# First batch of a cosformer attention and routed FFN kernel: the order of loading, scaling and summing is rearranged

## The chip, the cores and the metric

The kernel runs on one core of a Trainium2 chip. The metric is the device time of one execution in microseconds (us). Four runs of the kernel before took 980.68, 981.9, 982.14 and 980.2 us, a median of 981.29. One execution was recorded by the hardware profiler.

## The reference

A linear attention is followed by a soft mixture of eight experts. N = 8 x 576 = 4608 tokens of width 512 come out of the attention, and all experts work on all tokens, weighted by a matrix P that is balanced in eight steps.

```python
batch, n_heads, seq, head_dim = (8, 8, 576, 64)
theta = np.pi / 2.0 * pos / S
def phi(x, c, s):
    r = np.maximum(x, 0.0)
    return np.concatenate([r * c, r * s], axis=-1)
q_p = phi(q, cos_w, sin_w); k_p = phi(k, cos_w, sin_w)
kv = np.einsum('bhsf,bhsd->bhfd', k_p, v)
z = np.sum(k_p, axis=2)
num = np.einsum('bhsf,bhfd->bhsd', q_p, kv)
den = np.einsum('bhsf,bhf->bhs', q_p, z)[..., None] + 1e-06
x = (num / den)            # as (4608, 512)
P = np.exp(x @ w_gate)     # then 8 times: rows and columns normalized
for e in range(8):
    h = np.maximum(x @ w1[e], 0.0)
    out += P[:, e:e + 1] * (h @ w2[e])
```

## The kernel before

The chip's engines each run a stream of instructions in order: TensorE (PE), VectorE (DVE), ScalarE (ACT), GpSimd (POOL, here mostly the queue from which loads are issued) and SyncE (SP, here the queue of transposes and stores). The helpers te, ve and se record every operation in the order in which the source has it, so that the source order is the engines' order; that is why nearly all instructions of the profile carry line 109, and are told apart by the tiles that they write and read.

One core holds all of the attention's output as xT (512 columns on 4 x 128 partitions, by tokens). The attention runs batch by batch. Two heads form a pair hk (0 to 3), and a batch has two halves of two pairs each, one load for each of q, k and v and half, issued by `load` (L198). While batch b is attended to, expert 0's FFN works on tokens of the batches before: `ffn1` (L142, x by w1, relu into hT) and `ffn2` (L155). The list `todo`, filled at L651 to L728, hangs attention steps of later batches behind the FFN's slots. After the eighth batch come the other seven experts, from about 180 us to the end, in a form of Strassen's products; the change does not touch them.

Batch 0 has nothing to run beside, and its steps stand written out at L593 to L649. The names that matter:

- `load` order at L217 to L243: q0, then an iota (gidx, the positions) and a mask (ident, the identity), then q1, k0, k1, v0, v1, two quarters of w1, the two loads of batch 1's k, the other quarters, batch 1's q and v, and w2 in quarters. From the tenth load on, each waits for the one eight places ahead.
- `keep_busy(n)` (L245) gives TensorE matmuls whose result nobody reads, in all n x 128 columns wide. Before the first real work stand 74 of 128 columns.
- `cs` are the cosine and sine tables, made by ScalarE (L272); `cs_half` (L274 to L280) is a copy of the cosines of each half of the partitions, wanted by `key_sums`.
- `prep_q` (L346) multiplies a pair's q by cs on VectorE into q_p (a product of 128 x 1152; three buffers). `turn` (L389) transposes a third of that on TensorE into a bank of small_ps, of which there are four in rotation, and a relu takes it out into q_pT, on ScalarE for batch 0, alternately on ScalarE and VectorE for batch 1.
- `prep_k` (L339) is the relu of a pair's k in place, on VectorE for batch 0 and on either for batch 1; `prep_kp` (L375) its product with cs into k_p.
- `key_sums` (L412): z of a half's heads by 36 narrow matmuls straight from k; `key_sums_made` (L427) brings it into zsel on VectorE.
- `denominators` (L496): q_pT by zsel into one bank (three matmuls for each head), and with the last head the reciprocal `den`, its parts hi and hl, all on VectorE.
- `sums_begun` and `sums_made` (L446, L468): kv of a half by 36 matmuls into two banks, copied to kv_sb by ScalarE.
- `attend` (L531): for one pair, three matmuls spread hl over the partitions into two banks (rb_ps), ScalarE copies them to rb, four matmuls make the numerators into two more banks (num_ps), and VectorE multiplies both into xT.
- L623 to L647: four banks first_ps (two of h_ps, two of y_ps) collect the FFN's first four output tiles over kt = 0 to 3, each kt as soon as the pair hk = kt has been attended to, and then ScalarE takes the relus. `ffn1` of tile 4 and 5 uses the two banks of h_ps next.
- Between the attends stand the relus and products of batch 1's keys (L642 to L647), and behind them batch 1's q (L648).

The softmax here doesn't subtract the row's maximum and nothing guards it: scores larger than these inputs give would overflow.

## Time and profile before

| What | us |
|---|---|
| median of four runs | 981.29 |
| the profiled execution | 980.68 |
| its span, first to last instruction | 979.0 |

The stages of the profiled execution, with the busy time of each engine in them; a matmul's recorded length includes its way through the array, so that a busy PE is not a PE at its peak:

| us from the start | PE | DVE | ACT | POOL | GB/s |
|---|---|---|---|---|---|
| 0 to 8 | 6.86 | 4.12 | 4.12 | 6.79 | 94 |
| 8 to 16 | 7.99 | 5.94 | 4.81 | 4.59 | 191 |
| 16 to 24 | 7.75 | 6.43 | 4.83 | 4.07 | 203 |
| 24 to 34 | 8.24 | 7.47 | 8.62 | 4.52 | 206 |
| 34 to 44 | 10.00 | 7.35 | 5.58 | 0.00 | 184 |
| 44 to 80 | 34.79 | 27.62 | 23.62 | 8.57 | 161 |
| 80 to 180 | 100.00 | 66.62 | 60.02 | 14.50 | 128 |

The granted TensorE clock is 1.00 in each of them. Batch 0's own steps and batch 1's preparation fill the first 34 us. The loads of the start land one after another: q0 4.6 us after its issue at 1.31, q1 5.2 after 2.62, k0 7.3 after 3.39, k1 some 8 after 4.10. In these first microseconds PE is occupied by the 74 matmuls of 128 columns (1.14 to 7.94).

### The profile page before, as it was taken

To read this page: it belongs to the slowest core of one execution; us is meant where nothing else is said; L and a number is where in the kernel's file an instruction comes from. 1 tells how busy PE (TensorE), PEld (TensorE's weight loads), DVE (VectorE), ACT (ScalarE), POOL (GpSimd) and SP (SyncE) were. 2 spreads that over 40 slices of the span, in tenths; PEclk is the share of its full clock that TensorE was granted. 3 is DMA by queue.
4 is the path that set the end of the run, shared out by engine and by line. 5 is a ranking of instruction groups with operands and counts; after the bars stand their busy time and mean duration, and the time that the engine had idled before them with its cause. 6 is when DMAs were issued, how large, how long until landed. Compare 5 with 4: busy or idle time off the path is not lost.

```text
span 979.0 us, 20237 instructions
## 1 busy us (share of the span) xinstructions
PE 964.9 (99%) x7855; PEld 674.7 (69%) x7855; DVE 807.2 (82%) x1833; ACT 564.9 (58%) x1262; POOL 60.7 (6%) x82
## 2 busy tenths in 40 slices
PE   9999999999999999999999999999999999999997
PEld 6544454457777777777777777777777777777775
DVE  6767774888988888988888888988888888988887
ACT  5766665467776555555555555555555555555551
POOL 6231110010000000000000000000000000000001
PEclk9999999999999999999999999999999999999999
DMA  9999885330103401223103401223103401104435
GB/s 164 184 154 174 155 136 105 74 68 25 50 25 70 91 25 28 64 56 68 44 25 75 85 25 34 62 55 69 41 25 76 84 25 35 40 26 120 127 88 128
DMA packets 80336, 73.54 MB, mean 75 GB/s; under 512 B 33264, under 2 KB 72176, under 8 KB 80240
## 3 DMA queue, kind: packets, MB, share of 16 engines
q0 software_dynamic: 27232, 30.94, 20.3%
q1 hardware_dynamic: 52768, 41.06, 17.1%
q8 instruction: 61, 1.00, 0.4%
q14 instruction: 35, 0.29, 0.1%
q10 hardware_dynamic: 240, 0.26, 0.1%
HBM read 83.12 MB, written 12.98 MB: 98 GB/s over the span
## 4 chain that ended last, share of the span: by engine, by line
PE 88%; DMA 4%; DVE 3%; issue 2%; ACT 1%; POOL 1%; POOLq 0%; ACTq 0%; SPq 0%
PE rows_ps L109 33%; PE h_ps L109 26%; PE p_ps L109 11%; PE copied_ps L109 11%; PE y_ps L109 4%; PE small_ps L109 3%; DMA k_ld<-in_k_dram 1%; DMA w2e<-in_moe_w_dram 1%; DMA w1e<-in_moe_w_dram 1%; DMA acc_hi<-q_p 1%; DVE P_tok L109 1%; DVE colp L109 0%; POOL q_ld L202 0%; DVE rs L109 0%; DVE acc_hi L926 0%
## 5 line engine op out<-in xcount | busy, mean ns | idle before, releaser
L926 DVE SCALAR_TENSOR_TENSOR acc_lo<-rows_ps,P_tok,acc_lo 128x512 f32<-128x512 f32 (+1 forms) x322 | 203.5, 641 | 74.9 <-PE rows_ps L109 74.8
L109 PEld LDWEIGHTS <-H 128*128 128x128 f16 x2080 | 203.1, 98 | 82.5 <-issue 1.2
L862 ACT CAST u<-h_ps 128x384 f16<-128x384 f32 x288 | 137.8, 478 | 131.2 <-PE h_ps L109 131.2
L109 PEld LDWEIGHTS <-w1e 128*128 128x128 f16 x1632 | 157.3, 98 | 67.5 <-issue 5.9
L856 DVE CUSTOM_DVE_ANT_0 H<-p_ps,u 128x384 f16<-128x384 f32 x329 | 181.3, 551 | 6.4 <-PE p_ps L109 6.4
L109 PEld LDWEIGHTS <-hs 128*128 128x128 f16 x1500 | 146.6, 98 | 56.2
L109 PE MATMUL h_ps<-S,w1e 128*128 128x384 f16 x672 | 164.1, 326 | 0.7 <-ACT u L109 0.6
L109 PE MATMUL p_ps<-xT,T 128*128 128x384 f16 x672 | 164.1, 326 | 0.1
L109 PE MATMUL rows_ps<-V,H 128*128 128x256 f16 x1000 | 150.0, 273 | 0.7 <-DVE acc_hi L926 0.7
L109 PE MATMUL rows_ps<-w2e,hs 128*128 128x256 f16 x1000 | 150.0, 273 | 0.0
L109 PE MATMUL h_ps<-xT,w1e 128*128 128x384 f16 (+1 forms) x616 | 149.4, 350 | 0.3 <-DVE xT L109 0.2
L894 ACT ACTIVATE H<-h_ps 128x384 f16<-128x384 f32 x144 | 70.7, 491 | 95.0 <-PE h_ps L109 95.0
L109 PEld LDWEIGHTS <-T 128*128 128x128 f16 x1008 | 98.4, 98 | 29.9 <-issue 3.3
L109 PE MATMUL rows_ps<-w2e,H 128*128 128x256 f16 (+1 forms) x568 | 92.3, 285 | 0.0
L875 ACT COPY copied_ps<-h_ps 128x384 f32<-128x384 f32 x144 | 67.5, 468 | 35.2 <-PE h_ps L109 35.2
L885 ACT ACTIVATE H<-copied_ps 128x384 f16<-128x384 f32 x144 | 70.9, 492 | 20.3 <-PE copied_ps L109 20.3
L109 PE MATMUL h_ps<-S,T 128*128 128x384 f16 x336 | 81.8, 325 | 0.3 <-ACT copied_ps L109 0.3
L109 PE MATMUL copied_ps<-xT,w1e 128*128 128x384 f16 x336 | 82.1, 326 | 0.0
L109 PE MATMUL copied_ps<-w2e,H 128*128 128x256 f16 x504 | 75.5, 272 | 0.0
L109 PE MATMUL rows_ps<-V,hs 128*128 128x256 f16 x500 | 74.9, 272 | 0.0
L926 DVE SCALAR_TENSOR_TENSOR acc_lo<-copied_ps,P_tok,acc_lo 128x256 f32<-128x256 f32 x126 | 60.2, 478 | 0.4
L926 DVE SCALAR_TENSOR_TENSOR acc_hi<-rows_ps,P_tok,acc_hi 128x512 f32<-128x512 f32 (+1 forms) x56 | 41.3, 738 | 20.5 <-PE rows_ps L109 19.7
(145 smaller groups left out, 950.2 us busy)
## 6 DMA issues: line engine op xcount, KB each, us to landing
S<-x_saved SPq DMA_DIRECT2D x108, 192.0 KB, 2.4
out_dram<-acc_lo SPq DMA_DIRECT2D x62, 128.0 KB, 2.4
w1e<-in_moe_w_dram POOLq DMA_DIRECT2D x7, 1024.0 KB, 8.9
w2e<-in_moe_w_dram POOLq DMA_DIRECT2D x7, 1024.0 KB, 10.0
q_ld<-in_q_dram POOLq DMA_DIRECT2D x16, 288.0 KB, 6.4
k_ld<-in_k_dram POOLq DMA_DIRECT2D x16, 288.0 KB, 8.1
v_ld<-in_v_dram POOLq DMA_DIRECT2D x16, 288.0 KB, 9.4
x_saved<-S SPq DMA_DIRECT2D x18, 192.0 KB, 1.9
```

Of the source, the lines that this page charges most:

```text
L109: i = getattr(self.engine, name)(*args, **kwargs)
L856: latest = ve._custom_dve(TENSOR_ADD_SAT, out=out, in0=ps[:, 0:TU], in1=t[:], s0=FP32_MAX, s1=0.0)
L862: se.copy(out=t[:], in_=ps[:, 0:TU])
L875: se.copy(out=Y[:, 0:TU], in_=X[:, 0:TU])
L885: se.activation(out=h11, in_=Y[:, 0:TU], func=AF.Relu)
L894: se.activation(out=h12, in_=X[:, 0:TU], func=AF.Relu)
L926: ve.scalar_tensor_tensor(out=a, in0=rows, scalar=P_tok[:, g, self.e : self.e + 1], in1=a, op0=ALU.mult, op1=ALU.add,)
```

## The change

It rearranges batch 0 in these places:

1. POOL issues q0, q1, the iota, k0, the mask, k1, then as before.
2. `cs_half` is filled by a function `halve`, called behind the second q product instead of at once. Five small constants and the memsets of v_augs are made earlier.
3. All four q products stand ahead of the first relu of k (before, the fourth stood behind two relus).
4. Behind the turns come: the first key product, the first zsel, the two other key relus, the second key product, the first denominators, the second key sums, two wide fillers, the second zsel and denominators with the reciprocal, kv of half 0, five wide fillers, and only then the last two key products.
5. `attend` is split into `spread_out` and `numerators`. Pair 0 is attended to, two fillers follow, pair 1's spread, then kv of half 1, which goes into the two banks of h_ps instead of small_ps, two more fillers, and pair 1's numerators.
6. The four tiles of first_ps are worked on, and their relus taken, in the order 2, 3, 0, 1.
7. Batch 1's key relus on ScalarE (pairs 0 and 1) stand behind pair 3's copies, and all of batch 1's other key preparation behind the last attend.

The numbers of matmuls, relus and products stay the same but for the fillers (31 x 128 columns behind the turns before, 44 x 128 after).

```diff
         load(0, 0, "q")
+        load(0, 1, "q")
         gidx = cs_pool.tile([P, C], FP32, name="gidx")
...
+        load(0, 0, "k")
         ones_sq = cs_pool.tile([P, P], F16, name="ones_sq")
...
-        load(0, 1, "q")
-        for name in "kv":
-            load(0, 0, name)
-            load(0, 1, name)
+        load(0, 1, "k")
+        for half in range(2):
+            load(0, half, "v")
...
-        def sums_begun(b, half):
+        def sums_begun(b, half, banks=(ps_s, "small_ps")):
...
-            kv_ps = [ps_s.tile([P, 512], FP32, name="small_ps") for hh in range(2)]
+            kv_ps = [banks[0].tile([P, 512], FP32, name=banks[1]) for hh in range(2)]
...
         for hk in range(HK):
+            prep_q(0, hk)
+            if hk == 1:
+                halve()
             if hk == 3:
                 prep_k(0, 0)
                 prep_k(0, 1)
                 z_ps = key_sums(0)
-                prep_q(0, hk)
-                key_sums_made(0, z_ps)
-            else:
-                prep_q(0, hk)
             for i in range(3):
                 turn(0, hk, i, True)
                 keep_busy(3)
         prep_kp(0, 0)
+        key_sums_made(0, z_ps)
+        for hk in (2, 3):
+            prep_k(0, hk)
         prep_kp(0, 1)
         denominators(0, range(0, 4))
+        z_ps = key_sums(1)
         keep_busy(8)
+        key_sums_made(1, z_ps)
+        denominators(0, range(4, 8))
+        sums_made(0, 0, sums_begun(0, 0))
+        keep_busy(20)
         for hk in (2, 3):
-            prep_k(0, hk)
-        z_ps = key_sums(1)
-        prep_kp(0, 2)
-        key_sums_made(1, z_ps)
-        prep_kp(0, 3)
-        keep_busy(5)
-        denominators(0, range(4, 8))
-        for half in range(2):
-            sums_made(0, half, sums_begun(0, half))
-            keep_busy((0, 18)[half])
+            prep_kp(0, hk)
+        spread_out(0, 0)
+        numerators(0, 0)
+        keep_busy(8)
+        spread_out(0, 1)
+        sums_made(0, 1, sums_begun(0, 1, (ps_h[0], "h_ps")))
+        keep_busy(8)
...
         for hk in range(HK):
-            attend(0, hk)
+            if hk > 1:
+                spread_out(0, hk)
+            if hk:
+                numerators(0, hk)
+            if hk == 3:
+                prep_k(1, 0)
+                prep_k(1, 1)
             for kt in ((), (0,), (1,), (2, 3))[hk]:
-                for ft, h_ps in enumerate(first_ps):
+                for ft, h_ps in ((2, first_ps[2]), (3, first_ps[3]), (0, first_ps[0]), (1, first_ps[1])):
...
-            for i in ((), (0,), (1, 2), ())[hk]:
-                prep_k(1, i, i < 2)
-            for i in ((), (0,), (1,), (2, 3))[hk]:
-                if i == 3:
-                    prep_k(1, i, False)
-                prep_kp(1, i)
+        for hk in range(HK):
+            if hk >= 2:
+                prep_k(1, hk, False)
+            prep_kp(1, hk)
         for hk in range(3):
             prep_q(1, hk)
```

## The prediction

> **What bounds the kernel now.** I read the page first, then the stages, then each engine's timeline from 10 to 34 us, then who waits for whom after 34 us. The page says that over the whole span TensorE is the limit:

> ```profile
> PE 964.9 (99%) x7855; PEld 674.7 (69%) x7855; DVE 807.2 (82%) x1833; ACT 564.9 (58%) x1262; POOL 60.7 (6%) x82
> ```

> That average hides the start. The change touches only batch 0 and the preparation of batch 1, all before 34 us, and there the limit passes from engine to engine. VectorE (start, length, instruction, repeats, idle time before and its cause):

> ```profile
> 10.71 0.53 DVE L109 TENSOR_SCALAR k_ld<-k_ld 128x576 f16<-128x576 f16 x2 [1.78 <-DMA k_ld<-in_k_dram]
> 11.15 0.75 DVE L109 TENSOR_TENSOR q_p<-q_ld,acc_hi 128x1152 f16<-128x1152 f16 x1
> ...
> 15.82 1.35 DVE L109 RECIPROCAL den<-y_ps 96x192 f32<-96x192 f32 x1
> ...
> 17.50 0.41 DVE L109 SCALAR_TENSOR_TENSOR hl<-hi,lo,den 96x192 f16<-96x192 f16 x1
> 18.86 0.82 DVE L109 TENSOR_TENSOR xT<-small_ps,rb 128x384 f16<-128x384 f32 x2 [0.94 <-ACT rb L109]
> ...
> 24.96 0.30 DVE L109 TENSOR_SCALAR k_ld<-k_ld 128x576 f16<-128x576 f16 x1
> 25.29 0.76 DVE L109 TENSOR_TENSOR k_p<-k_ld,acc_hi 128x1152 f16<-128x1152 f16 x1
> 25.96 2.09 DVE L109 TENSOR_TENSOR q_p<-q_ld,acc_hi 128x1152 f16<-128x1152 f16 x3
> 27.97 0.55 DVE L109 TENSOR_SCALAR q_pT<-small_ps 128x384 f16<-128x384 f32 x1
> 28.44 0.75 DVE L109 TENSOR_TENSOR q_p<-q_ld,acc_hi 128x1152 f16<-128x1152 f16 x1
> 29.11 0.56 DVE L109 TENSOR_SCALAR q_pT<-small_ps 128x384 f16<-128x384 f32 x1
> ```

> The reader is to see prices here (a product of 1152 takes 0.75 us, but three take 2.09, so they start 0.67 apart; a relu with its product takes 0.33 more), and that VectorE goes without idle time from the first batch-1 products to the eviction at 29.11. TensorE and ScalarE in the same stretch:

> ```profile
> 17.97 0.42 PE L109 MATMUL small_ps<-hl,acc_hi 96*128 96x192 f16 x3
> ...
> 19.47 0.57 PE L109 MATMUL small_ps<-q_pT,kv_sb 128*64 128x384 f16 x4
> ...
> 24.42 0.59 PE L109 MATMUL h_ps<-xT,w1e 128*128 128x512 f16 x2 [0.24 <-DVE xT L109]
> 25.48 1.89 PE L109 MATMUL h_ps<-xT,w1e 128*128 128x512 f16 x8
> 27.21 0.67 PE L109 MATMUL small_ps<-ident,q_p 128*128 128x128 f16 x9
> ```

> ```profile
> 24.84 1.08 ACT L109 ACTIVATE hT<-h_ps 128x512 f16<-128x512 f32 x2 [1.34 <-PE h_ps L109]
> ...
> 26.76 1.24 ACT L109 ACTIVATE hT<-h_ps 128x512 f16<-128x512 f32 x2
> ...
> 32.54 0.73 ACT L109 COPY acc_lo<-v_ld 128x576 f16<-128x576 f16 x1
> ```

> From 24.84 to 33.27 us ScalarE has no idle row over 0.02 us: whatever delays the first relu of hT, or makes a hole behind it, delays the copy at 32.54, the key sums of batch 1 that wait for it, and all that follows.

> **The change part by part.** Loads: on POOL's queue q1 is issued ahead of the iota and k0 ahead of the mask. Each issue is some 0.72 us, so the iota and with it the cosine tables come 0.72 us later (3.67 instead of 2.95, done by 5.0), and q0 lands only at 5.9 (issue 1.31 plus 4.6 to landing): hidden, cost 0; without that cover it would be 0.72. VectorE begins q_p near 5.9 instead of 6.83, as it no longer waits for the table to fill cs_half. But TensorE's 74 warm-up matmuls and the three epsilon products end at 8.33, and the turns start there before and after: gain 0. No DMA of SP's moves.

> q ahead of k: the fourth q_p runs near 9.4 instead of 11.15, and the first key product takes its place. TensorE's row is unchanged to 13.16, because k0 lands at 10.68 and the key sums stand between the turns. What is gained is 0.67 us of VectorE. The next two key relus then run at 12.4 instead of 13.72, and the second key sums follow the first denominators at 13.60 without a wait, where they began at 14.14. Second denominators, reciprocal and hl come 0.5 us earlier: reciprocal 15.3, hl done 17.4, spread at 17.45 instead of 17.97. **So far -0.5.** Five fillers of 0.22 stand under the reciprocal, free while it lasts.

> The two key products now follow hl: 17.35 to 18.7 (0.67 + 0.75). The first xT multiplication, ready at 18.35, waits for them: 18.7 instead of 18.86. TensorE meanwhile: spread 0.35, numerators 0.37, two fillers 0.43, spread 0.34, half of 72 key-value products (1.15 us from 15.71 to 16.86) 0.58, two fillers 0.43, which is 2.50. Second numerators at 17.45 + 2.50 = 19.95 instead of 19.47: **the head start is gone and +0.45 stands.** The numerators take 0.37 instead of 0.50 (their bank is free by then), so the first h matmuls run at 20.3 for 19.97. Two rounds of 1.585 follow, unchanged. The last xT pair no longer stands behind a key product: 0.51 us after its rb copy (as 18.35 to 18.86) instead of 0.76, so it ends at 24.46 and kt = 3 starts at 24.5 for 24.42: **+0.1.** ScalarE's two key relus, moved here, take 23.7 to 25.0 and meet the first hT relu at 24.92.

> Now two things come late. First, ffn1(4) takes the buffer of first_ps[0], whose relu is now third of four: relus start 0.48 apart and last 0.60, so it is free 1.57 us after the first at 24.95, at 26.5 instead of 25.43. ffn1(4) starts at 26.55, **+1.1**; ffn1(5) and the turns of batch 1 queue behind it (1.73 us for the eight), so the turns start at 28.3 at the earliest. Secondly, batch 1's key preparation was spread between the xT pairs and now follows the last one: four products and two relus, 4 x 0.67 + 2 x 0.33 = 3.34 from 24.45, so q_p of batch 1 starts at 27.8 instead of 25.96, **+1.85**, and ends at 28.54; turns at 28.6 for 27.21. The two delays overlap. VectorE then repeats its old rows: 2.0 for the products, evictions and the fourth q_p as before, last eviction over at 31.5 (29.67). Its bank is what the last part of the third turn needs, so that TensorE gets to ffn1(7) at 31.7 instead of 30.13, its relu to 32.9 instead of 31.31 and the v copy to 34.1 instead of 32.54. **Sum +1.6 us.**

> One row speaks of the moved relus: one took 0.51 instead of 0.30, just while POOL issued a load.

> ```profile
> 22.15 0.72 POOL L133 DMA_DIRECT2D w2e<-in_moe_w_dram  x1 [0.63 <-DMA w1e<-in_moe_w_dram]
> ...
> 22.47 0.51 DVE L109 TENSOR_SCALAR k_ld<-k_ld 128x576 f16<-128x576 f16 x1
> ```

> [...]

> Bounds from rows: a relu between 0.30 and 0.51, so 0 to +0.4 for two; k0 landing moves nothing up to 0.3 either way. After 34 us every transfer that TensorE waits for is issued by the engines' own progress, so the delay should pass undiminished; the waits there that a DMA makes are small (the second stands behind a key relu on ScalarE that waits for a load):

> ```profile
> PE small_ps L109 <- DMA acc_hi<-q_p: 0.4, 1, 0.4
> PE small_ps L109 <- ACT rb L109: 0.4, 1, 0.4
> ```

> Both could go or grow when loads and transposes meet differently: -0.9 to +0.5.

> The profiled execution took 980.68 us (span 979.0), 0.6 below the median of 981.29. Forecast for it 982.3, for the median **982.9**. A measurement of this kernel tells about 0.2%, 1.96 us, from no change, so 979.33 to 983.25 counts as the same.

> **The rivals.** (B) The head start survives: batch 1's keys and ffn1(4) have cover I don't see. For it: reciprocal and hl really come 0.5 earlier. Against it: the unbroken ScalarE and VectorE rows. -0.5, 980.8; it would show q_p of batch 1 by 26.0. (C) Slower beyond 0.2%: the two delays add instead of overlapping. Evictions of the turned q alternate between ScalarE (1.1 late) and VectorE (1.85 late) through four banks, and TensorE, in order, waits for each in turn: 1.1 + 1.85 = 2.95, 984.2. For it: the 0.40 us that TensorE waits for such a bank already at 29.80, and relus of 0.51. Against it: by my sum ffn1(5) ends only 0.3 before q_p is ready. It decides if the turns start after 29.4. (D) B, and the two DMA-made waits go, because batch 2's loads end at 43.2 (the last issued at 32.51, 10.6 to landing) whatever the engines do and the transposes meet an empty queue: -0.5 - 0.9 = -1.4, 979.9. Against it: B's failing.

> **How the numbers follow.** Forecast 0.50, with its own range of 982.2 to 983.6 (a quarter of it beyond 983.25); C 0.27; B 0.17; D 0.06. Slower: 0.27 + 0.13 = 0.40; faster: most of D, as a spread of 0.5 between runs lies about it, 0.05; same 0.55. The range reaches down to B and up past C by 0.3: 980.7 to 984.5.

> **What would show it.** Right: reciprocal near 15.3; second numerators near 19.95; a hole of about 1.1 us on TensorE between kt = 3 and ffn1(4); q_p of batch 1 near 27.8; the v copy near 34.1, and the same 1.6 at the end. Wrong: the keys' products finding room between the xT pairs, a first turn before 8.3, or a delay at 34 us that is made good before 80.

## The result, and the profile after

| | us |
|---|---|
| median before, 54 runs beside the changed kernel's | 981.17 |
| median after, 33 runs | 983.45 |
| ratio, 95% interval | 1.0026 (1.0018 to 1.0034) |

The change costs 2.28 us, a quarter of a per cent. (The ratios here and below are as recorded; they are not the quotient of the two medians.) The forecast was 982.9 with its own range of 982.2 to 983.6; the median lies in it, 0.2 us beyond the line that was drawn for "the same". The profiled execution of the changed kernel took 988.53 us (span 986.8), where 982.3 was forecast for it, and is no typical one: it contains a stall at 74 us that 8 of the 33 runs may share (they lie above 984.5 us). Its first 70 us can be read like the others.

TensorE's timeline of the changed kernel, from the reciprocal to batch 1 (start and length in us, then what is written and read, in brackets the idle time ahead and what ended it):

```profile
17.17 0.42 PE L109 MATMUL small_ps<-hl,acc_hi 96*128 96x192 f16 x3 [0.47 <-DVE hl L109]
17.52 0.44 PE L109 MATMUL small_ps<-q_pT,kv_sb 128*64 128x384 f16 x4
17.89 0.61 PE L109 MATMUL y_ps<-ones_sq 128*128 128x512 f16 x2
18.33 0.41 PE L109 MATMUL small_ps<-hl,acc_hi 96*128 96x192 f16 x3
18.68 0.70 PE L109 MATMUL h_ps<-v_ld,k_p 64*128 64x64 f16 x36
19.31 0.61 PE L109 MATMUL y_ps<-ones_sq 128*128 128x512 f16 x2
19.84 0.44 PE L109 MATMUL small_ps<-q_pT,kv_sb 128*64 128x384 f16 x4
...
24.46 0.59 PE L109 MATMUL y_ps<-xT,w1e 128*128 128x512 f16 x2
24.89 0.59 PE L109 MATMUL h_ps<-xT,w1e 128*128 128x512 f16 x2
26.50 1.89 PE L109 MATMUL h_ps<-xT,w1e 128*128 128x512 f16 x8 [1.01 <-ACT hT L109]
28.53 0.68 PE L109 MATMUL small_ps<-ident,q_p 128*128 128x128 f16 x9
```

The reader sees the spread at 17.17 (17.97 before), then the fillers and half of the key-value sums ahead of the second numerators, which so come at 19.84 (19.47 before): the head start is gone within 2.7 us. The hole of 1.01 us ahead of ffn1(4) is the bank of first_ps[0]. VectorE in the same stretch:

```profile
16.70 0.41 DVE L109 SCALAR_TENSOR_TENSOR hl<-hi,lo,den 96x192 f16<-96x192 f16 x1
17.03 1.42 DVE L109 TENSOR_TENSOR k_p<-k_ld,acc_hi 128x1152 f16<-128x1152 f16 x2
18.37 0.81 DVE L109 TENSOR_TENSOR xT<-small_ps,rb 128x384 f16<-128x384 f32 x2
20.31 0.82 DVE L109 TENSOR_TENSOR xT<-small_ps,rb 128x384 f16<-128x384 f32 x2 [1.13 <-PE small_ps L109]
21.96 0.82 DVE L109 TENSOR_TENSOR xT<-small_ps,rb 128x384 f16<-128x384 f32 x2 [0.83 <-ACT rb L109]
23.55 0.85 DVE L109 TENSOR_TENSOR xT<-small_ps,rb 128x384 f16<-128x384 f32 x2 [0.76 <-ACT rb L109]
24.35 1.43 DVE L109 TENSOR_TENSOR k_p<-k_ld,acc_hi 128x1152 f16<-128x1152 f16 x2
...
27.72 1.42 DVE L109 TENSOR_TENSOR q_p<-q_ld,acc_hi 128x1152 f16<-128x1152 f16 x2
```

VectorE now idles 1.13 + 0.83 + 0.76 = 2.72 us between the xT pairs, just where the kernel before did batch 1's key products (two of its rows):

```profile
20.67 0.75 DVE L109 TENSOR_TENSOR k_p<-k_ld,acc_hi 128x1152 f16<-128x1152 f16 x1
...
22.90 0.74 DVE L109 TENSOR_TENSOR k_p<-k_ld,acc_hi 128x1152 f16<-128x1152 f16 x1
```

The changed kernel does these from 24.35 on: q_p of batch 1 starts at 27.72 instead of 25.96. ScalarE has holes where it had none, and the v copy that was at 32.54 is at 34.06:

```profile
27.56 0.60 ACT L109 ACTIVATE hT<-h_ps 128x512 f16<-128x512 f32 x1 [0.62 <-PE h_ps L109]
28.42 0.60 ACT L109 ACTIVATE hT<-h_ps 128x512 f16<-128x512 f32 x1 [0.27 <-PE h_ps L109]
...
30.11 0.60 ACT L109 ACTIVATE hT<-h_ps 128x512 f16<-128x512 f32 x1 [0.33 <-PE h_ps L109]
...
34.06 0.69 ACT L109 COPY acc_lo<-v_ld 128x576 f16<-128x576 f16 x1
```

**The stall.** TensorE's waits of the changed kernel in the first 100 us (total, times, longest) begin with a transfer, and the timelines of SyncE's and GpSimd's queues and of TensorE, and the windows (PE, weight loads, VectorE, ScalarE and GpSimd busy, then the granted clock), show how it came about:

```profile
PE small_ps L109 <- DMA acc_hi<-q_p: 4.3, 1, 4.3
```

```profile
68.21 1.51 SPq L365 DMA_TRANSPOSE acc_hi<-q_p  x1
...
68.03 1.43 POOL L202 DMA_DIRECT2D q_ld<-in_q_dram  x2 [11.44 <-DVE acc_lo L109]
...
78.27 0.51 PE L109 MATMUL small_ps<-acc_hi,zsel 128*32 128x192 f16 x6 [4.32 <-DMA acc_hi<-q_p]
```

```profile
78.00:80.00 2.00, 1.73 (x10) 0.60 (x10) 1.14 (x2) 0.00 (x0) 0.00 (x0) 0.50 1.20 202
80.00:82.00 2.00, 2.00 (x6) 0.73 (x5) 1.90 (x5) 0.60 (x1) 0.00 (x0) 0.50 1.21 206
...
84.00:86.00 2.00, 2.00 (x15) 0.93 (x13) 0.74 (x3) 1.74 (x5) 0.00 (x0) 1.00 1.27 212
```

The last transposition of batch 3 was issued 0.18 us behind the first of six loads and landed 10.0 us later (6.2 before, 0.11 us behind). TensorE stood still for 4.32 us, and worked at half its clock (0.50) until about 84 us. On the trace's own clock the changed kernel is 1.52 us behind the one before at 72 us and 7.86 from 89 us on. That is one question that the experiments had to answer: how much of the median's 2.28 us is made there?

**How the traces are compared.** The 74 warm-up matmuls do not take the same time in each execution: the first turn starts anywhere between 7.33 and 8.61 us in the thirteen profiles of this study that have all 74, and just as widely in the eight of them with the same code up to there. 0.44 us of what the changed kernel's profile shows as earlier is this luck (first turn at 7.89, 8.33 before). So in what follows a shift is a start in the kernel's trace less that in the trace before, less the same difference for the first turn. Columns: the spread, the second numerators, the first q_p of batch 1, its first turn, and the relu of hT that ran at 50.73 us before; the last column is the median less that of the kernel before measured beside it.

| kernel | first turn at | spread | 2nd num. | q_p | turn | relu at 50.73 | median |
|---|---|---|---|---|---|---|---|
| changed | 7.89 | -0.37 | +0.81 | +2.20 | +1.76 | +1.92 | +2.28 |
| e1, keys back | 8.36 | -0.46 | +0.72 | +0.40 | +1.35 | +1.35 | +1.27 |
| e2, tile order back | 8.55 | -0.44 | +0.74 | +2.12 | +1.69 | +1.85 | +1.47 |
| e3, both back | 7.84 | -0.30 | +0.88 | +0.54 | +0.54 | +0.53 | +0.53 |
| e3f, and no fillers | 8.61 | -0.46 | -0.02 | -0.33 | -0.33 | -0.34 | +0.26 |
| w1, front alone | 8.02 | -0.43 | -0.43 | -0.63 | -0.64 | -0.63 | -0.27 |
| p6, order alone | 8.53 | 0.00 | 0.00 | +0.02 | +0.99 | +0.99 | +1.79 |

### The profile page after: what moved, and what is told of

Its sections match the earlier page's. It is cut to its first block, busy times and chain, and to the rows that moved or that the text cites. A ratio compares the mean times of both kernels' runs of the same rounds, so it can differ in the third digit from the quotient of the medians.

```text
span 986.8 us, 20241 instructions
## 1 busy us (share of the span) xinstructions
PE 967.6 (98%) x7857; PEld 674.7 (68%) x7857; DVE 808.1 (82%) x1833; ACT 565.4 (57%) x1262; POOL 60.4 (6%) x82
## 3 DMA queue, kind: packets, MB, share of 16 engines
q0 software_dynamic: 27232, 30.94, 20.3%
q1 hardware_dynamic: 52768, 41.06, 17.4%
## 4 chain that ended last, share of the span: by engine, by line
PE 88%; DMA 5%; DVE 3%; issue 2%; ACT 1%; POOL 1%; POOLq 0%; ACTq 0%; SPq 0%
PE rows_ps L109 33%; PE h_ps L109 26%; PE p_ps L109 11%; PE copied_ps L109 11%; PE y_ps L109 4%; PE small_ps L109 3%; DMA k_ld<-in_k_dram 1%; DMA w2e<-in_moe_w_dram 1%; DMA w1e<-in_moe_w_dram 1%; DMA acc_hi<-q_p 1%; DVE P_tok L109 1%; DVE colp L109 0%; POOL q_ld L202 0%; DVE rs L109 0%; DVE acc_hi L949 0%
## 5 line engine op out<-in xcount | busy, mean ns | idle before, releaser
L109 PEld LDWEIGHTS <-H 128*128 128x128 f16 x2080 | 203.1, 98 | 82.5 <-issue 1.2
L109 PEld LDWEIGHTS <-w1e 128*128 128x128 f16 x1632 | 157.8, 98 | 69.9 <-issue 9.3
L109 PEld LDWEIGHTS <-hs 128*128 128x128 f16 x1500 | 146.6, 98 | 56.2
L109 PE MATMUL h_ps<-S,w1e 128*128 128x384 f16 x672 | 164.1, 326 | 0.7 <-ACT u L109 0.6
L109 PE MATMUL p_ps<-xT,T 128*128 128x384 f16 x672 | 164.1, 326 | 0.1
L109 PE MATMUL h_ps<-xT,w1e 128*128 128x384 f16 (+1 forms) x616 | 151.7, 355 | 1.0 <-ACT hT L109 1.0
L109 PE MATMUL rows_ps<-V,H 128*128 128x256 f16 x1000 | 150.0, 273 | 0.7 <-DVE acc_hi L949 0.7
L109 PE MATMUL rows_ps<-w2e,hs 128*128 128x256 f16 x1000 | 150.0, 273 | 0.0
L109 PEld LDWEIGHTS <-T 128*128 128x128 f16 x1008 | 98.4, 98 | 29.9 <-issue 3.3
L109 PE MATMUL rows_ps<-w2e,H 128*128 128x256 f16 (+1 forms) x568 | 92.3, 285 | 0.0
L908 ACT ACTIVATE H<-copied_ps 128x384 f16<-128x384 f32 x144 | 70.9, 492 | 20.3 <-PE copied_ps L109 20.3
L109 PE MATMUL h_ps<-S,T 128*128 128x384 f16 x336 | 81.8, 325 | 0.3 <-ACT copied_ps L109 0.3
L109 PE MATMUL copied_ps<-xT,w1e 128*128 128x384 f16 x336 | 82.1, 326 | 0.0
L109 PE MATMUL copied_ps<-w2e,H 128*128 128x256 f16 x504 | 75.5, 272 | 0.0
L109 PE MATMUL rows_ps<-V,hs 128*128 128x256 f16 x500 | 74.9, 272 | 0.0
```

The source lines that it names most:

```text
L109: i = getattr(self.engine, name)(*args, **kwargs)
L908: se.activation(out=h11, in_=Y[:, 0:TU], func=AF.Relu)
```

## The experiments

**Undoing one of the two late things, and both.** First the keys alone (e1), the tile order alone (e2), both (e3).

```diff
# e1 against the changed kernel
-            if hk == 3:
-                prep_k(1, 0)
-                prep_k(1, 1)
...
-        for hk in range(HK):
-            if hk >= 2:
-                prep_k(1, hk, False)
-            prep_kp(1, hk)
+            for i in ((), (0,), (1, 2), ())[hk]:
+                prep_k(1, i, i < 2)
+            for i in ((), (0,), (1,), (2, 3))[hk]:
...
# e2 against the changed kernel (e3 has both)
-                for ft, h_ps in ((2, first_ps[2]), (3, first_ps[3]), (0, first_ps[0]), (1, first_ps[1])):
+                for ft, h_ps in enumerate(first_ps):
```

> The changed kernel with batch 1's key relus and products put back between the attends, as in the kernel before; the order 2, 3, 0, 1 of the first four FFN tiles stays. The changed kernel is 2.3 us slower than before, and 1.5 us of that stand on TensorE at 34 us. Theory (the two late things, VectorE's products and the bank that ffn1(4) waits for, lie beside each other): VectorE is early again (q_p of batch 1 near 26.0 to 26.5 us instead of 27.72), but ffn1(4) still waits about 1 us behind kt = 3 and the turns queue behind it, so only some 0.45 us comes back: +1.5 to +2.1 us over before. Rival 1 (the two delays add): all of the 1.8 us of VectorE comes back, +0.2 to +0.7. Rival 2 (the loss is made where transposes and loads meet at 66 to 78 us, not in the first batch): nothing comes back, +2.0 to +2.6, with ffn1(4) and the v copy early in the trace.

> The changed kernel with the first four FFN tiles in the order 0, 1, 2, 3; the key preparation of batch 1 stays behind the last attend. Theory (delays beside each other): the 1 us hole ahead of ffn1(4) goes (it starts near 25.5 us), but q_p of batch 1 still starts near 27.7 us, TensorE waits there instead, and the v copy stays near 34: 0 to 0.2 us back, +2.0 to +2.4 over before. Rival 1 (the delays add): about 1.0 us back, +1.2 to +1.4. Rival 2 (the loss comes from transposes and loads at 66 to 78 us): nothing back, +2.0 to +2.6; here theory and rival 2 look alike, and the run with both parts undone tells them apart.

> Both undone: the key preparation of batch 1 between the attends and the tiles in the order 0, 1, 2, 3; all of the rest of the change stays (loads, q ahead of k, the split attends, half of the key-value sums behind the first numerators). Theory (delays beside each other): more comes back than by the two alone together, 1.4 us: +0.6 to +1.2 us over before; v copy near 32.7 us. Rival 1 (the delays add): 2.8 us back, -0.6 to -0.2. Rival 2 (transposes and loads at 66 to 78 us): within 0.4 us of the changed kernel, +2.0 to +2.6.

Medians: e1 982.82, e2 983.02, e3 982.08 against 981.55 before; ratios 1.0013 (1.0004 to 1.0022), 1.0021 (1.0009 to 1.0033), 1.0004 (0.9992 to 1.0016). Taken alone the medians do not bear the theory out: e1 (+1.27) and e2 (+1.47) lie under its ranges (1.5 to 2.1 and 2.0 to 2.4), e2 nearly in the range of the rival by which the delays add (1.2 to 1.4), and e3 (+0.53) just under 0.6. TensorE's timelines of e1, e2 and e3, one after the other, tell more:

```profile
26.87 1.89 PE L109 MATMUL h_ps<-xT,w1e 128*128 128x512 f16 x8 [1.02 <-ACT hT L109]
28.60 0.67 PE L109 MATMUL small_ps<-ident,q_p 128*128 128x128 f16 x9
```

```profile
26.10 1.89 PE L109 MATMUL h_ps<-xT,w1e 128*128 128x512 f16 x8
29.12 0.68 PE L109 MATMUL small_ps<-ident,q_p 128*128 128x128 f16 x9 [1.12 <-DVE q_p L109]
```

```profile
25.53 1.89 PE L109 MATMUL h_ps<-xT,w1e 128*128 128x512 f16 x8
27.25 0.67 PE L109 MATMUL small_ps<-ident,q_p 128*128 128x128 f16 x9
```

With the keys back, q_p is there (26.40), but the bank's hole of 1.02 us stands and the turns queue behind ffn1(4) and (5). With the tile order back the hole is gone from ffn1(4) and reappears, 1.12 us long, ahead of the turns: q_p is late. Only with both back is there no hole. In the table, over e3's +0.53 at the relu: order alone (e1) +0.82, keys alone (e2) +1.32, both +1.39. They lie beside each other; a sum would be 2.14. The medians gave back 1.0, 0.8 and 1.75 us, which looks like a sum, but each is uncertain by more than half a us; this was tried again below.

**The order alone, in the kernel before (p6).**

```diff
# against the kernel before
-                for ft, h_ps in enumerate(first_ps):
+                for ft, h_ps in ((2, first_ps[2]), (3, first_ps[3]), (0, first_ps[0]), (1, first_ps[1])):
```

> The kernel before with one line of the change alone: the four first FFN tiles in the order 2, 3, 0, 1. Theory (the bank of first_ps[0] is freed third, ffn1(4) waits, and the turns of batch 1 queue behind ffn1(4) and ffn1(5) with only 0.1 us of slack against q_p): a hole of about 1.0 us ahead of ffn1(4), turns at 28.1 to 28.3 us instead of 27.21, +0.7 to +1.1 over before. Rival (the hole is harmless by itself, because evictions and the v copy bind behind it): within 0.3 us of before, with the hole in the trace.

983.02 against 981.23, ratio 1.0018 (1.0006 to 1.0029). The theory's hole and its price on the turns came as said:

```profile
26.68 1.89 PE L109 MATMUL h_ps<-xT,w1e 128*128 128x512 f16 x8 [1.02 <-ACT hT L109]
28.41 0.67 PE L109 MATMUL small_ps<-ident,q_p 128*128 128x128 f16 x9
```

The shift is 0.99 us, and stays so until 54 us. The median is higher than that, and than the 0.7 to 1.1 expected (+1.79, with an interval of about +0.6 to +2.8); the profiled execution waits 1.8 us for the same last transposition.

**The fillers (e3f).** What is left in e3 is +0.88 us at the second numerators.

```diff
# against e3
         numerators(0, 0)
-        keep_busy(8)
         spread_out(0, 1)
         sums_made(0, 1, sums_begun(0, 1, (ps_h[0], "h_ps")))
-        keep_busy(8)
```

> The kernel with both undone (tiles in order, batch 1's keys between the attends), and besides without the two groups of two wide fillers between pair 0's numerators and pair 1's. Theory (what is left of the loss sits on TensorE between the first and the second numerators, and 0.86 us of it are fillers): the second numerators 0.6 to 0.9 us earlier against the spread, 0.4 to 0.9 us off the time of the kernel with both undone, so -0.4 to +0.1 against before. Rival (VectorE's two key products and its xT bind there, and the fillers only fill a hole): the time of the kernel with both undone, +0.3 to +0.7 over before.

981.49 against 981.23, ratio 0.9999 (0.9985 to 1.0012). The second numerators' shift goes from +0.88 to -0.02, that at 50 us from +0.53 to -0.34: 0.87 to 0.90 us, nearly all of the 0.44 + 0.53 that they took. So they stood on the path, though not all of it comes back there: from the spread to the second numerators e3f takes 1.93 us where e3 took 2.68, which is 0.75 of the 0.97, and 0.22 turns into short waits between the steps; the rest of the 0.90 is the spread, 0.16 earlier in e3f's trace. The total follows only in part: -0.27 against e3, which such medians cannot tell from -0.87, and +0.26 over before, between the theory's range (-0.4 to +0.1) and the rival's (+0.3 to +0.7).

**The front alone (w1).** The loads, q ahead of k and the early key sums of the changed kernel, with the last two key products ahead of the second denominators, and everything behind the reciprocal as before.

```diff
# against the changed kernel, beside what e3 undoes
+        prep_kp(0, 2)
         key_sums_made(1, z_ps)
         denominators(0, range(4, 8))
+        prep_kp(0, 3)
-        sums_made(0, 0, sums_begun(0, 0))
-        keep_busy(20)
-        for hk in (2, 3):
-            prep_kp(0, hk)
...
+        for half in range(2):
+            sums_made(0, half, sums_begun(0, half))
+            keep_busy((0, 18)[half])
```

> The changed kernel's front (loads, all q ahead of k, second key sums early; the last two key products ahead of the reciprocal, where they need no wait) with the tail of the kernel before (both halves' key-value sums under the reciprocal, whole attends, batch 1's key preparation between them, tile order 0 to 3). Theory (the head start of 0.5 us at the reciprocal is real, and the tail of the change lost it): 0.4 to 0.9 us faster than before, with the spread near 17.2 us and the second numerators near 18.8; this one beats both kernels. Rival 1 (the head start has no cover behind it and is lost at batch 1's loads or at ScalarE's unbroken run): within 0.2 us of before. Rival 2 (an earlier first batch makes the transposes of later batches meet their loads worse): +0.5 or more in spite of an earlier v copy.

981.28 against 981.55, ratio 0.9995 (0.9976 to 1.0013): undecided by the median. The trace has the theory's rows (spread 17.23, second numerators 18.73) and a head start of 0.63 us at 50 us, and shows where it goes. ScalarE's timeline, TensorE's, and a window with the granted clock:

```profile
57.75 0.68 ACT L109 ACTIVATE k_ld<-k_ld 128x576 f16<-128x576 f16 x1 [2.56 <-DMA k_ld<-in_k_dram]
```

```profile
59.34 0.46 PE L109 MATMUL small_ps<-hl,acc_hi 96*128 96x192 f16 x3 [1.43 <-ACT rb L109]
```

```profile
60.00:62.00 2.00, 2.00 (x8) 0.56 1.50 98
```

The relu of batch 3's k waits on ScalarE for its load; the copies rb of the next attend stand behind it; TensorE stands for 1.43 us and then gets 0.56 of its clock. In the kernel before the same relu started at 57.78, though everything around it was 0.94 us later on the trace's own clock: w1 came early and waited for a load that took 6.42 us instead of 5.51. From 89 us on its trace is 0.66 us behind that of the kernel before.

**The two meetings moved (b2, w2).** The k relu goes behind the next attend's copies, batch 4's loads are held back behind one more xT pair, and batch 4's first k relu goes one slot on; in the kernel before (b2) and in w1 (w2).

```diff
-                    (4, prep_q, 0), (5, prep_q, 1), (8, prep_k, 0), (8, prep_q, 2),
+                    (4, prep_q, 0), (5, prep_q, 1), (8, prep_q, 2), (9, prep_k, 0),
...
-                    (4, prep_q, 0), (5, prep_k, 0), (5, prep_q, 1), (6, prep_k, 1),
+                    (4, prep_q, 0), (5, prep_q, 1), (6, prep_k, 0), (6, prep_k, 1),
...
-                        at(j, 12, load, b + 2, half, name, True)
+                            at(j, 13, load, b + 2, half, name, True)
```

> The kernel before with two steps of later batches moved, its first batch as it was. The relu of batch 3's first k, for which ScalarE stands 1.57 us at 57.8 us until its load has landed, comes behind the copies of the next attend; the loads of batch 4 are held back behind pair 3's xT products, about 0.7 us later, so that they are issued after batch 3's last transposition (0.11 us ahead of it before), and batch 4's first k relu moves by one slot. Theory (both are places where TensorE waits for a transfer, 0.4 us each in the trace before and up to 4.3 us in the changed kernel's): -0.4 to -0.9 against before, and no run over 984. Rival (the loads land 0.7 us later and something else waits for them): within 0.3 us of before, or slower.

> The changed kernel's front with the tail of the kernel before, and the two steps of later batches moved. In the profile of the front alone the head start on TensorE was 0.94 us until 55 us, and at 57.8 us ScalarE stood 2.56 us behind the k load of batch 3 and the head start was gone. Theory (the head start is lost there, to a transfer with a time of its own, and passes once nothing waits for it): 0.5 to 0.7 us faster than the kernel before with the same two steps moved, -1.0 to -1.6 against before. Rival (the front gains nothing; its 0.94 us was the luck of one execution's warm-up): equal to the kernel before with the two steps moved.

Against 981.23: b2 980.94, ratio 0.9993 (0.9985 to 1.0002), highest of 12 runs 981.94; w2 980.71, ratio 0.9990 (0.9982 to 0.9999), highest of 11 runs 981.13. The gain of b2 is smaller than expected (0.29), and not shown by its interval; what changed is the tail. w2 is the fastest of all, 0.52 us under the kernel before where 1.0 to 1.6 were expected; of the front's 0.5 to 0.7 us against b2 the medians show 0.23, which lies within their noise. VectorE's timeline of w2 shows where the front was stopped in that execution:

```profile
27.43 0.76 DVE L109 TENSOR_TENSOR q_p<-q_ld,acc_hi 128x1152 f16<-128x1152 f16 x1 [1.14 <-DMA q_ld<-in_q_dram]
```

Batch 1's second q load landed at 27.40 (25.60 in w1). It is the fourteenth in a row of loads of which most land some 1.4 us behind the one before; this one took 2.9.

**The change with the meetings moved (a2), and each late thing undone there (a2e1, a2e2).** The edits are those of b2, with none, with e1's and with e2's.

> The changed kernel, whole, with the two steps of batches 3 and 4 moved as in the kernel before with them moved (which was 0.3 us faster than before, and its runs lay within 2.2 us). So its time against that one is the first batch's own price, without the meeting of transposition and loads at 66 to 78 us. Theory (the loss is made in the first 34 us): +1.3 to +1.8 over before, 1.6 to 2.0 over the kernel before with the steps moved, no run over 985. Rival (a good part of the 2.3 us is made at 66 to 78 us): +0.4 to +1.0 over before.

> The same, with batch 1's key preparation back between the attends, the tile order 2, 3, 0, 1 kept. In the first four experiments the medians gave back 1.0 us for the keys alone, 0.8 for the tile order alone and 1.8 for both, which looks like a sum; the traces up to 55 us, set against the first turn, gave 0.56, 0.07 and 1.38, which does not. Here the runs spread less. Theory (beside each other): 0.4 to 0.7 us faster than the changed kernel with the steps moved. Rival (they add): 0.9 to 1.2 faster.

> The same, with the tiles in the order 0, 1, 2, 3 and the key preparation behind the last attend. Theory (beside each other: q_p of batch 1 is late anyway): 0 to 0.2 us faster than the changed kernel with the steps moved. Rival (they add): 0.7 to 1.0 faster.

Against 981.31: a2 982.46, ratio 1.0013 (1.0004 to 1.0021); a2e1 981.97, 1.0009 (0.9998 to 1.0020); a2e2 982.54, 1.0008 (0.9996 to 1.0020). a2 lies 0.1 to 0.2 under the theory's numbers, at +1.15 over before and +1.15 + 0.29 = 1.44 over b2, and above the rival's (0.4 to 1.0); its interval, about +0.4 to +2.1 us, excludes neither. No run is over 983.28. The keys alone give back 0.49 us (0.4 to 0.7 expected), the tile order alone nothing (-0.08): beside each other, not added, now in the medians too, though these two differences are each uncertain by about one us, so that here too the traces decide. The shifts at 50 us repeat those of the first three kernels of the table to 0.2: a2 +2.09, a2e1 +1.40, a2e2 +1.83 (a2's is some 0.25 too high: its turns began at 7.33, VectorE then waited 0.88 us for the first k, and the spread's shift is only -0.20). The group of transpositions (DMA issues from 60 to 90 us, median us to landing) was

```profile
acc_hi<-q_p SPq DMA_TRANSPOSE x1, 10.0
```

in the changed kernel's profile, and in a2's, where it was issued 0.60 us ahead of the first load,

```profile
acc_hi<-q_p SPq DMA_TRANSPOSE x1, 5.1
```

Of the six kernels with the meetings moved (w3 below is the sixth) none of 67 runs is above 984.5 us; of the seven rearranged ones without, 17 of 104, 8 of them the changed kernel's 33; of the kernel before, 8 of 157. The profiles point the same way: the three that took over 984.5 us (changed, e2, e3) are the three in which TensorE waits longest for this transposition (4.32, 2.88 and 2.24 us) and then gets half its clock (granted 0.50). In e2 and e3:

```profile
77.81 0.35 PE L109 MATMUL small_ps<-acc_hi,zsel 128*32 128x192 f16 x6 [2.88 <-DMA acc_hi<-q_p]
```

```profile
75.79 0.35 PE L109 MATMUL small_ps<-acc_hi,zsel 128*32 128x192 f16 x6 [2.24 <-DMA acc_hi<-q_p]
```

In all six profiles with the meetings moved the transposition is issued 0.52 to 1.91 us ahead of the first load, and it lands within 5.2 us. So the tail goes with this meeting. Two steps were moved together, though, and the k relu's share was not tried by itself; nor were the kernels with and without the moves all timed beside each other. Why the changed kernel meets the stall more often than the one before is open.

**Fewer warm-up matmuls (w3).** The forecast put the earlier q loads at nothing, since the 74 matmuls hold the turns.

```diff
# against w2
-        for _ in range(74):
+        for _ in range(60):
```

> The changed kernel's front with the tail of the kernel before and the two later steps moved (981.23 before, 980.71 this, in the last call), with 60 warm-up matmuls instead of 74: it computes the same. The earlier q loads make q_p ready at 6.7 us, while the turns wait for the 74 until 7.7 to 8.6. Theory (from 8 to 44 us the loads land one after another at some 205 GB/s, 1.4 us each, and a front that is earlier meets batch 1's q load, which in the last run landed at 27.40 and stopped the turns): turns start 0.5 to 0.8 us earlier, and of that at most 0.3 us reaches the end. Rival (the warm-up bounds the front and nothing behind it does): 0.5 to 0.8 us faster than with 74.

980.94 against 981.31, ratio 0.9995 (0.9987 to 1.0004): no better than w2's -0.52. The turns start at 7.13, and VectorE then waits for the first k:

```profile
10.17 0.53 DVE L109 TENSOR_SCALAR k_ld<-k_ld 128x576 f16<-128x576 f16 x2 [0.75 <-DMA k_ld<-in_k_dram]
```

The spread comes at 16.84 (17.01 in w2): of 0.54 us at the first turn 0.17 is left there. Behind the warm-up the next bound, the loads' landing, is only some tenths away. What was left of the lead did not end there: until 54 us w3's trace runs 1.34 us ahead of the kernel before, more than any other. It is lost later, when VectorE waits 2.26 us for a transposition of q_p and TensorE behind it,

```profile
66.29 0.46 PE L109 MATMUL small_ps<-acc_lo,k_p 64*128 64x65 f16 x18 [1.77 <-DVE acc_lo L109]
```

and the clock is at half from 66.9 to 70.3 us; from 89 us on the trace is 0.12 us behind.

## Why the prediction was right, point by point

| Step | forecast | measured, against the first turn |
|---|---|---|
| loads: turns start unchanged | 0 | 0 by definition (not tested: the warm-up's own 1.3 us hides it) |
| spread | -0.5 | -0.37 (-0.46 to -0.20 in the eight traces with the same code up to there) |
| second numerators | +0.45 | +0.81 |
| kt = 3 | +0.1 | +0.48 |
| ffn1(4) | +1.1 | +1.46 (hole 1.01) |
| q_p of batch 1 | +1.85 | +2.20 |
| turns of batch 1 | +1.4 | +1.76 |
| ffn1(7) | +1.6 | +2.00 |
| v copy | +1.6 | +1.96 |

- **The step that was mis-sized** is "second numerators at 19.95 instead of 19.47". All that follows it is off by the same 0.35 to 0.4 us, and no later step adds to it. Two things make it up. hl and with it the spread came 0.15 us later than said, and from spread to second numerators TensorE took 19.84 - 17.17 = 2.67 us instead of 2.50: the fillers stand 0.44 and 0.53 apart from what follows, not 0.43 each, and half of the key-value sums took 0.63, not 0.58. e3f shows that this stretch is the path: without the fillers 0.87 of their 0.97 us comes back at 50 us.
- **There was luck in the numbers.** The profile has the v copy at 34.06 where 34.1 was forecast, since a warm-up 0.44 us shorter hid the 0.35. The median is 0.67 us above the forecast's +1.6 and only 0.15 under the upper end of its range: the mis-sized step and what may have come from the meetings both pushed up, and the range was just wide enough.
- **The mechanism held.** Keys behind the last xT pair, the bank freed third, their overlap (forecast +1.4 at the turns, from 1.85 and 1.1): shown by e1, e2, e3 and p6: in e1, e2 and p6 the hole stood where the theory put it, and in e3 there was none. (One reading was too round: VectorE had 0.31 us of idle time ahead of the xT pair at 21.73, so its unbroken run in the kernel before begins there and not with the first products of batch 1.) Rival C (they add, 2.95) would have had the turns after 29.4; they came at 28.53 (28.97 with the warm-up of the kernel before). Rival B (the head start survives) and D fell at the same row; w1 and e3f show that the head start was real and what lost it.
- **"The delay passes undiminished"** held from 34 to 72 us (1.36 to 1.52 us on the trace's own clock). Behind that the step failed as far as it called the later waits small. They were priced at -0.9 to +0.5; in the changed kernel's profile one of them is 4.3 us and the clock drops with it (0.50 from 77.04 to 83.87 us). Other profiles show that a shift in the first batch is not simply carried to the end: between 54 and 90 us w1's goes from -0.94 to +0.66, w3's from -1.34 to +0.12, and a2's, with the meetings moved, from +1.10 to +0.34. In the median it matters less: with both meetings moved the change costs 1.44 us instead of 2.28. The 0.84 between them is of the size of the intervals, so whether that part of the median comes from the meetings stays open; that the tail goes with them the runs and profiles show, without telling the two moved steps apart.
- **The stretched relu** (0.51 us at 22.47 before, begun 0.31 us into an issue of 0.72 on GpSimd) did not come: both moved relus took 0.30. One began 0.2 us before an issue and the other fell between two, so neither began inside one as that relu did. Other relus of the same size did: in the changed kernel one of batch 0 that began at 12.16, 0.44 us into an issue of 0.83, took 0.49. In the fourteen profiles those that began 0.29 to 0.49 us into an issue took 0.33 to 0.55 and ended 0.81 to 0.94 us after its start; those that began earlier or later in one kept 0.30 or 0.31. So the price in the prediction is real, but in these profiles a relu paid it only when it started 0.29 to 0.49 us into an issue; what makes it longer no run shows.

## What to carry to other kernels

Cover that is handed back must be looked for on the other engine: putting work behind an earlier step freed TensorE's and VectorE's queue for 0.4 us, and left VectorE idle for 2.7 us between steps whose gaps had held the next batch's products. When two delays lie beside each other, undoing either alone gives little, so a trial undoes both, and each alone, before a theory is dropped. And a gain of a few tenths in front of a queue of loads can end at the next load or transposition to land (w1, w2 and w3, each at another one); look there before trimming what bounds the start.
